# Linear attention and a multiplicative feed-forward on one core: w_out in four pieces, batch 0 first on two queues, and the whole sequence of steps as a list

## Chip, core and metric

The kernel runs on one core of a Trainium2 chip, in one launch. The metric is the device time in microseconds (us), from start to end of the program; lower is better. Each time of the kernel before is one execution; three were taken. The profile is of a fourth one.

## The reference

Eight batches of 8 heads, 576 tokens and 64 columns go through a linear attention, and its 4608 tokens of 512 columns through a feed-forward with no nonlinearity but one product:

```python
q_s = softmax(q, axis=head_dim)
k_s = softmax(k, axis=sequence)
kv  = einsum('bhsd,bhse->bhde', k_s, v)
x   = einsum('bhsd,bhde->bhse', q_s, kv)     # then (4608, 512)
h   = ((x @ w1) * (x @ w2)) @ w3             # 512 -> 1024 -> 1024
out = h @ w_out                              # 1024 -> 512
```

Everything comes in and goes out as float32.

## The kernel before

The kernel multiplies the two last weights first (W3O = w3 @ w_out, "the fold"), so each token needs only `x @ w1`, `x @ w2`, a product and one matmul with W3O. All matmuls are in float16.

**Steps.** The program is a set of named steps, each with one engine, a length and needs. `b` is a batch, `c` a chunk of 512 tokens (chunk 8 has the last 64 tokens of each batch), `p` one of two parts of the tokens of a batch (part 0 has 4 of 9 blocks, part 1 has 5), `hp` a pair of heads, `ft` one of 8 row blocks of w3.

- Loads: `k.b`, `q.b` (or `q.b.p`), `v.b`; `w3.r` (r = 0 to 3 one row block, 4 and 5 two each), `wo.i` (w_out), `w1.i` and `w2.i` (quarters of the columns). The loads that GpSimd (POOL) issues go through its own queue and cast the weights to float16; at most eight are under way, so each waits for the one eight before it. The others are issued by SyncE (SP), and in the kernel before one by ScalarE (ACT).
- Fold: `w3t.ft` (8 transposes on TensorE, PE), `w3T.ft` (copy to SBUF), `pf.ft.h` (matmuls with w_out, in pieces `h`), `W3O.ft` (scaled copy). Lines 430 to 455.
- Keys: `kmx` (max over tokens, on VectorE, DVE; as a tree of four max operations or as two reduces), `cb` (the max shared between partitions), `ksub`, `kexp`, `vc` (cast of v, batch 2 on), `kv` (matmuls), `kv2` (division).
- Queries: `qmx`, `qsub`, `qexp`, `qsm`, `qeps`, `qrc`, `qn`; then the transposed copy, by PE and a copy (`qt`, `qT`; batches 0 and 1) or by a DMA that transposes (`qd` on SP; batch 2 on). `xm`, `xt` are the matmuls with kv2, `xs`, `xts` their copies into the chunk's x.
- Feed-forward: `up.1` and `up.0` (x @ w2, x @ w1), `bs` (copy of the first to SBUF), `ab` (product, DVE), `down` (matmul with W3O), `os` (copy to SBUF), `st` (store, SP). Chunk 1 is done in two halves of 256 tokens.

**What sets the order.** `Plan` (lines 18 to 163) walks the steps with its own model: at each point it takes the engine that can begin first, and on it the ready step that is worth most, from the length of the chain behind it and a table of leads (`LEADS`). Each engine then executes its instructions in exactly this order: an instruction that waits holds all that come after it on its engine. `PICKS` says which engine does a step that two could do.

**Rings.** PSUM has four banks `pab` (w3t, up), two `po` (pf, down) and two `att` (the attention). A step that takes a bank waits until the one that had it before has been copied away. Two buffers `w3T`, four `osb` and four `bsb` go round in the same way.

**Ports.** For steps that the model puts before 50 us (`LINKED`), DVE and POOL steps that would want the same SBUF port are put one behind the other by hand (`link`).

**Start.** 35 matmuls on zeros (`WARM`, line 331) run ahead of the first real work on PE.

Of the kernel before, what the change touches and what calls it, by code (L numbers as in the profile page):

```python
# [17 lines left out]
class Plan:  # L18


    RATE = 409.0e3
# [3 lines left out]
    LINKED = 50.0  # L25
    BUS = 2.2
    BEGIN = {"SP": 0.74, "POOL": 1.25, "DVE": 1.0, "ACT": 0.74, "PE": 1.0}

    def __init__(self, rings, leads, picks):
        self.rings = rings  # L30
        self.leads = leads
        self.picks = picks
        self.steps = {}
# [53 lines left out]
    def order(self):  # L87
# [23 lines left out]
        order = []  # L111
        while ready:
            could = {}
            for s in ready:
# [17 lines left out]
            ready.remove(s)  # L132
            if s["takes"]:
                fifo[s["takes"]] += [s["name"]] * s["slots"]
# [30 lines left out]

LEADS = {
    "W3O_0": 3.86, "W3O_1": 96.54, "W3O_2": 83.51, "W3O_3": -17.88, "ab_0": -0.11, "ab_1": -73.36,
    "ab_3": 34.13, "bs_0": -13.75, "bs_1": 26.85, "cb_0": -28.89, "cb_1": -63.79, "cb_3": 85.84,
    "down_0": 18.28, "down_1": 46.89, "down_2": 9.08, "down_3": 7.55, "kexp_0": 74.7,
    "kexp_1": 91, "kexp_2": -24.67, "kexp_3": 36.31, "kmx_0": 45.3, "kmx_1": 45.3, "kmx_2": 3.5,  # L170
    "kmx_3": -326.21, "ksub_0": -8.7, "ksub_1": 43.5, "ksub_2": 11.41, "kv2_0": -31.5,
    "kv2_2": 9.92, "kv2_3": 9.95, "kv_0": -23.87, "kv_2": 73.56, "kv_3": 1.56, "os_0": 21,
    "os_1": 33.3, "pf_0": -14.77, "pf_1": -39.98, "qT_0": -24.5, "qT_1": 4.7, "qd_3": 74.8,
    "qeps_0": 28.2, "qeps_1": 75.9, "qeps_2": 37.85, "qeps_3": 10.34, "qexp_0": -32.3,
    "qexp_1": 16, "qexp_2": 53.74, "qmx_0": 53.9, "qmx_1": 35.3, "qmx_2": -27.61,
    "qmx_3": -327.82, "qn_0": 35, "qn_1": 67, "qn_2": 7.08, "qn_3": 52.76, "qrc_0": 4.6,
    "qrc_1": 72.9, "qrc_2": -5.55, "qrc_3": 10.13, "qsm_0": 39.4, "qsm_1": -10.4,
    "qsm_3": -119.37, "qsub_0": 33, "qsub_1": 46.8, "qsub_2": 4.33, "qsub_3": 56.82, "qt_0": 19.6,
    "qt_1": -23.5, "up0_0": -35.85, "up0_2": 29.56, "up0_3": 18.58, "up1_0": 34.45,
    "up1_1": -5.77, "up1_2": 83.41, "up1_3": 2.63, "vc_0": -11, "vc_1": 88.7, "vc_2": 14.71,  # L180
    "vc_3": -62.31, "w3T_1": -15.99, "w3T_2": -15.02, "w3T_3": 15.55, "w3t_0": 16.91,
    "w3t_1": -1.07, "w3t_2": 91.42, "w3t_3": -34.54, "xm_0": 13, "xm_1": 71, "xm_3": 40.96,
    "xs_0": -10.9, "xs_1": 40.6, "xs_2": -39.44, "xt_1": -8.76, "xt_2": 87.37, "xts_0": 92.5,
    "xts_1": 21.3, "xts_2": 20.18, "kexp_1_0": -3.8, "kmx_0_0": 35.13, "kmx_1_0": 10.95,
    "ksub_0_0": 67.6, "ksub_1_1": 98.9, "kv2_0_0": 66.1, "kv2_0_1": -22.4, "kv2_1_0": -4.2,
    "kv2_1_1": -2.9, "qT_0_0": -16.99, "qT_0_16": -45.54, "qT_1_16": 14.03, "qT_1_8": 84.36,
    "qeps_0_0": 62, "qeps_1_1": -9.58, "qexp_0_0": -10.92, "qexp_0_1": 44.82, "qexp_1_0": 37.04,
    "qexp_1_1": 87.94, "qmx_0_1": 81.93, "qmx_1_0": 3.1, "qmx_1_1": 40.66, "qn_0_1": 59.43,
    "qn_1_0": 17.44, "qrc_0_0": -5.67, "qrc_0_1": 56.34, "qrc_1_0": -35.48, "qrc_1_1": 61.9,
    "qsm_0_0": -32.45, "qsm_0_1": -0.84, "qsm_1_0": 111.27, "qsm_1_1": 32.24, "qsub_1_1": 51.26,  # L190
    "qt_0_8": 117.57, "qt_1_16": 50.48, "xm_0_0": -8.96, "xm_1_0": 37.69, "xs_0_0_0": 126.04,
    "xs_0_1_0": 22.27, "xs_1_0_0": 68.42, "xs_1_0_1": -20.74, "xs_1_1_0": -5.29,
    "xs_1_1_1": 24.82, "xts_0_0": 87.6, "xts_1_0": 44.57, "xts_1_1": 0.91, "pf_3": 93.65,
    "qt_1_8": 41.11, "xts_3": 61.7, "up0_1": -35.55, "xs_0_0_1": 38.71, "qd_2": -6.42,
    "qeps_1_0": 43.3, "xm_1_1": 15.9, "bs_3": 17.21, "ksub_3": 60.61, "kexp_0_1": -29.34,
    "xs_3": -18.62, "ksub_1_0": 40.77, "kv_1": -27.68, "qsm_2": -10.85, "os_3": 33.24,
    "qeps_0_1": -20.17, "qn_1_1": -32.16, "xt_0": -10.26, "w3T_0": 10.76, "kv2_1": -50.89,
    "pf_2": 21.11, "kexp_0_0": -3.81, "qT_1_0": 30.3, "qn_0_0": 8.76, "qt_0_0": -12.93,
    "qt_1_0": 70.46, "ab_2": 10.05, "qsub_0_1": 76, "xs_0_1_1": -39.93, "qT_0_8": 89.83,
    "xt_3": 59.16, "kexp_1_1": -11.89, "ksub_0_1": -14.41, "qexp_3": 1.21, "qmx_0_0": 70.49,  # L200
    "bs_2": 86.82, "cb_2": -45.47, "qsub_0_0": 70.81, "qsub_1_0": 31.62, "qt_0_16": -45.2,
    "xm_0_1": 58.68, "xts_0_1": 96.24,
# [36 lines left out]


LOADS = [
    ("q", 0, 1), ("q", 0, 0), ("w3", 4), ("wo", 0), ("k", 0), ("w3", 3), ("wo", 1), ("w3", 0),
    ("w3", 1), ("q", 1, 0), ("v", 0), ("w3", 5), ("k", 1), ("w3", 2), ("w2", 0), ("k", 2),
    ("w1", 0), ("w2", 2), ("w2", 1), ("w1", 1), ("w1", 2), ("v", 1), ("w1", 3), ("w2", 3),
    ("q", 1, 1),
]


@with_exitstack
def kernel(  # L250
    ctx: ExitStack,
    tc: tile.TileContext,
    q: bass.AP,
    k: bass.AP,
# [52 lines left out]
    st = {}  # L307
# [619 lines left out]
```

## Time and profile before

| what | value |
| --- | --- |
| median of 3 runs | 245.56 us (245.14 to 246.42) |
| the profiled execution | 246.21 us |
| its span, first to last instruction | 244.4 us |
| PE busy | 235.3 us (96%) |
| DVE, ACT, POOL busy | 177.2, 124.2, 118.9 us |
| PE at the head: matmuls on zeros | 1.55 to 12.06 us |
| first x @ w2 / first x @ w1 on PE | 37.62 / 38.93 us |

An engine's row in a timeline has the start, the length, the operation, and in brackets how long the engine was idle ahead of it and who ended this. "DMA to landing" is the time from the issue of a transfer to the end of it. The profiled execution is 1.8 us longer than its span, and 0.65 us above the median.

### The profile page before, as it was taken

The numbers are of one execution on the slowest core, as the hardware profiler recorded it, in microseconds if no ns is written. First come the engines' busy times: TensorE is split into PE (matmuls) and PEld (weight loads), VectorE is DVE, ScalarE is ACT, GpSimd is POOL, SyncE is SP. The second block draws the span as 40 slices with busy tenths as digits, with TensorE's granted clock in tenths as the row PEclk, the third lists the DMA queues.
The fourth block names the chain that finished last, engine by engine and source line by source line (L and its number), as shares of the span: only waits on it lengthen the run. The fifth ranks groups of instructions, "written<-read, shape, count | busy, mean of one in ns | idle before, by whom it ended". The sixth has DMA issues, their size and how long they took to land.

```text
span 244.4 us, 4841 instructions
## 1 busy us (share of the span) xinstructions
PE 235.3 (96%) x1919; PEld 115.1 (47%) x1919; DVE 177.2 (72%) x303; ACT 124.2 (51%) x189; POOL 118.9 (49%) x76
## 2 busy tenths in 40 slices
PE   7967999999999999999999999999999999999994
PEld 2444644457658344444444444444444344444443
DVE  0879799789889889898998899799965115573210
ACT  0374787468588357575565566655443612202221
POOL 8356789589791577086656646764470000000000
PEclk9999999999999999999999999999999999999999
DMA  6999999999999964985997299600830115000343
GB/s 206 266 253 251 305 299 199 240 371 352 395 401 232 215 132 144 398 152 117 339 317 153 46 361 326 150 14 4 188 80 3 43 43 130 1 0 0 87 130 129
DMA packets 37894, 45.66 MB, mean 187 GB/s; under 512 B 15984, under 2 KB 22384, under 8 KB 37872
## 3 DMA queue, kind: packets, MB, share of 16 engines
q1 hardware_dynamic: 29552, 33.69, 48.3%
q0 software_dynamic: 7792, 11.14, 20.7%
q10 hardware_dynamic: 528, 0.52, 0.6%
q8 instruction: 15, 0.25, 0.4%
q14 instruction: 7, 0.06, 0.1%
HBM read 38.80 MB, written 9.44 MB: 197 GB/s over the span
## 4 chain that ended last, share of the span: by engine, by line
PE 82%; DVE 5%; DMA 5%; POOL 4%; SPq 1%; ACT 1%; issue 1%; POOLq 0%; ACTq 0%
PE pab L786 48%; PE po L808 20%; PE po L444 4%; PE po L823 3%; PE pkv L555 2%; POOL en L620 2%; DMA q<-in_q_dram 2%; DMA qT<-en 2%; PE xm L661 2%; POOL q L588 2%; DVE q L588 1%; SPq L643 1%; DVE qm L583 1%; DVE qr L601 1%; PE w3t L434 1%
## 5 line engine op out<-in xcount | busy, mean ns | idle before, releaser
L801 DVE TENSOR_TENSOR ab<-pab,bsb 128x512 f16<-128x512 f32 x72 | 49.1, 686 | 29.4 <-PE pab L786 23.6
L786 PE MATMUL pab<-x,w2sb 128*128 128x512 f16 (+1 forms) x288 | 65.9, 356 | 0.0
L786 PE MATMUL pab<-x,w1sb 128*128 128x512 f16 (+1 forms) x288 | 65.9, 356 | 0.0
L808 PE MATMUL po<-W3O,ab 128*128 128x512 f16 x256 | 59.3, 380 | 0.0
L620 POOL TENSOR_TENSOR en<-eq,qr 128x1024 f16<-128x1024 f16 (+1 forms) x16 | 33.9, 2125 | 32.4 <-DVE qr L613 15.9
L342 ACT CAST bsb<-pab 128x512 f16<-128x512 f32 x42 | 24.6, 585 | 46.3 <-PE pab L786 36.8
L530 POOL TENSOR_TENSOR k<-k,cb 128x1152 f32<-128x1152 f32 x15 | 39.2, 2627 | 15.2 <-DVE cb L499 7.4
L786 PEld LDWEIGHTS <-w2sb 128*128 128x128 f16 x320 | 30.6, 98 | 29.9 <-issue 0.2
L786 PEld LDWEIGHTS <-w1sb 128*128 128x128 f16 x320 | 30.7, 98 | 29.5
L342 ACT COPY osb<-po 128x512 f32<-128x512 f32 (+1 forms) x33 | 19.1, 580 | 36.9 <-PE po L808 19.7
L808 PEld LDWEIGHTS <-ab 128*128 128x128 f16 x256 | 23.9, 98 | 29.3 <-issue 2.9
L588 POOL TENSOR_TENSOR q<-q,qm 128x1280 f32<-128x1280 f32 (+1 forms) x13 | 27.6, 2141 | 8.0 <-DVE qm L583 8.0
L342 DVE CAST bsb<-pab 128x512 f16<-128x512 f32 x30 | 20.4, 682 | 8.8 <-PE pab L786 7.8
L472 DVE TENSOR_REDUCE km<-k 128x128 f32<-128x1152 f32 x12 | 25.4, 2121 | 0.2 <-DMA k<-in_k_dram 0.2
L583 DVE TENSOR_REDUCE qm<-q 128x16 f32<-128x1024 f32 (+1 forms) x16 | 21.4, 1343 | 5.3 <-DMA q<-in_q_dram 5.2
L601 DVE TENSOR_REDUCE qr<-eq 128x16 f32<-128x1024 f16 (+1 forms) x16 | 21.2, 1329 | 2.4 <-ACT eq L596 2.4
L596 ACT ACTIVATE eq<-q 128x1024 f16<-128x1024 f32 (+1 forms) x16 | 18.6, 1164 | 5.6 <-POOL q L588 4.4
L538 ACT ACTIVATE ek<-k 128x1152 f16<-128x1152 f32 x16 | 18.6, 1165 | 5.5 <-POOL k L530 3.0
L346 ACT ACTIVATE x<-xm 128x512 f16<-128x512 f32 x29 | 16.2, 596 | 6.9 <-PE xm L661 6.8
L444 PE MATMUL po<-wosb,w3T 128*128 128x512 f16 x64 | 15.3, 380 | 2.0 <-ACT w3T L342 1.6
L342 ACT CAST v<-v 128x1152 f16<-128x1152 f32 x11 | 12.4, 1162 | 2.3 <-DMA v<-in_v_dram 2.3
L368 PE MATMUL idle<-zero 128*128 128x512 f16 x35 | 10.5, 475 | 1.6 <-DVE zero L365 1.6
(62 smaller groups left out, 166.7 us busy)
## 6 DMA issues: line engine op xcount, KB each, us to landing
out_dram<-osb SPq DMA_DIRECT2D x66, 128.0 KB, 2.5
q<-in_q_dram SPq DMA_DIRECT2D x6, 1152.0 KB, 9.2
v<-in_v_dram SPq DMA_DIRECT2D x6, 1152.0 KB, 11.6
k<-in_k_dram SPq DMA_DIRECT2D x5, 1152.0 KB, 5.5
k<-in_k_dram POOLq DMA_DIRECT2D x3, 1152.0 KB, 11.8
v<-in_v_dram POOLq DMA_DIRECT2D x2, 576.0 KB, 14.9
w<-in_moe_w_dram POOLq DMA_DIRECT2D x2, 512.0 KB, 11.9
wosb<-in_moe_w_out_dram POOLq DMA_DIRECT2D x2, 512.0 KB, 11.7
```

The source lines that it names most:

```text
L342: return [(nc.scalar.copy if eng == "ACT" else engine[eng].tensor_copy)(out=out, in_=in_)]
L444: nc.tensor.matmul(st["pf", ft], lhsT=st["w3T", ft][:, gt, :], rhs=wosb[:, gt, :], start=(gt == 0), stop=(gt == N_FT - 1))
L472: dve.tensor_reduce(out=st["km", b][:, two(hp), :], in_=kb[:, two(hp), :, :].rearrange("p h j d -> p h d j"), axis=AX.X, op=ALU.max)
L530: return [engine[eng].tensor_tensor(out=kb[:, two(hp), :, :], in0=kb[:, two(hp), :, :], in1=st["cb", b][:, two(hp), None, :].broadcast_to( ...
L538: nc.scalar.activation(out=st["ek", b][:, hp, :, :].rearrange("p j (i d) -> p i j d", i=2), in_=kb[:, two(hp), :, :], func=AF.Exp)
L583: dve.tensor_reduce(out=st["qm", b][:, :, j], in_=qb[:, :, j, :], axis=AX.X, op=ALU.max)
L588: return [engine[eng].tensor_tensor(out=qb[:, :, j, :], in0=qb[:, :, j, :], in1=st["qm", b][:, :, j, None].broadcast_to([P, HH, n, D]), op ...
L601: dve.tensor_reduce(out=st["qr", b][:, :, slice(*PARTS[p])], in_=st["eq", b, p], axis=AX.X, op=ALU.add)
L620: return [engine[eng].tensor_tensor(out=st["en", b][:, j, :, :].rearrange("p j h d -> p h j d"), in0=st["eq", b, p], in1=st["qr", b][:, :, ...
L786: nc.tensor.matmul(st["p", one, c, sub, u][:, a * (t1 - t0):(a + 1) * (t1 - t0)], lhsT=w[:, ct, fb * P:(fb + 1) * P], rhs=x()[:, ct, t0:t1 ...
L801: dve.tensor_tensor(out=st["ab", c][:, nf * u:nf * u + nf, t0:t1], in0=cut(st["p", 0, c, sub, u]), in1=cut(st["bsb", c, sub, u]), op=ALU.mult)
L808: nc.tensor.matmul(st["po", c, tb], lhsT=st["ab", c][:, ft, tb * P:(tb + 1) * P], rhs=W3O[:, ft, :], start=(ft == 0), stop=(ft == N_FT - 1))
```

## The change

- **w_out** comes in four pieces (`WOS = 4`), and a row block of the fold in four quarters of two matmuls. Its accumulator is in `po` for even and in `pab` for odd blocks.
- **k and q of batch 0**: `k.0` and `q.0.0` are split by heads into halves, one from SP and one from ACT. `q.0.1` goes to POOL's queue. The other loads of POOL have a new order, and `k.2` is the last of them; `q.2` on SP still waits for the third last of the list, now `w2.3`.
- **The sequence** of all 788 steps is written out in `ORDER`; the model only takes the next name. `LEADS` loses its use for the order, and many `PICKS` change: of the copies `bs`, 30 were on DVE and now one is, the others are on ACT.
- Batches 2 and 3 take `kmx` as a tree too (`TREES` 2 to 4), and `link` holds to 60 us.
- **24 matmuls on zeros** in place of 35.

```diff
-    def __init__(self, rings, leads, picks):
+    def __init__(self, rings, leads, picks, first):
...
+        self.first = [tuple(int(x) if x.isdigit() else x for x in n.split(".")) for n in first.split()]
...
+        listed = [steps[n] for n in self.first]
         while ready:
             could = {}
-            for s in ready:
+            for s in listed[:1] or ready:
+                assert not s["open"], s["name"]
...
+            listed = listed[1:]
...
+ORDER = """
+k.0 q.0.0 w3.4 wo.2 wo.1 wo.0 w3.5 wo.3 q.0.1 w3.2 ident kmx.0.0 qmx.0.0 w3.0 w3t.4 cb.0 w3t.5
+qsub.0.0 w3T.4 w3T.5 v.0 ksub.0.1 qexp.0.0 w3.3 pf.4.0 k.1 qsm.0.0 pf.5.0 pf.4.1 pf.5.1 ksub.0.0
+pf.4.2 pf.5.2 w3.1 w3t.7 qeps.0.0 kexp.0.0 qrc.0.0 w3t.6 qn.0.0 q.1.0 pf.4.3 pf.5.3 w3T.6 qt.0.0
+qmx.0.1 q.1.1 W3O.4 pf.6.0 pf.6.1 W3O.5 pf.6.2 w3T.7 w2.0 pf.6.3 qsub.0.1 w3t.2 kexp.0.1 pf.7.0
+w1.0 pf.7.1 w3T.2 pf.7.2 qexp.0.1 w3t.0 pf.2.0 pf.7.3 qT.0.0 qsm.0.1 pf.2.1 w2.1 pf.2.2 W3O.6
+kv.0 w3T.0 qeps.0.1 qrc.0.1 qn.0.1 pf.2.3 W3O.7 kv2.0 pf.0.0 w3t.3 W3O.2 pf.0.1 w3T.3 pf.0.2 w1.1
+qt.0.16 qt.0.8 kmx.1.0 qT.0.16 w2.2 pf.0.3 qT.0.8 pf.3.0 w1.3 w3t.1 pf.3.1 w3T.1 xm.0.0 w1.2
+pf.3.2 xs.0.0.0 xs.0.0.1 pf.3.3 pf.1.0 qmx.1.0 W3O.3 xm.0.1 w2.3 pf.1.1 xs.0.1.1 pf.1.2 xs.0.1.0
+qsub.1.0 pf.1.3 qmx.1.1 up.1.0.0.0 xt.0 bs.0.0.0 up.0.0.0.0 v.1 cb.1 W3O.1 up.1.0.0.1 qsub.1.1
+qexp.1.0 up.0.0.0.1 bs.0.0.1 ab.0.0.0 up.1.0.0.2 ab.0.0.1 ksub.1.0 qexp.1.1 up.0.0.0.2 qsm.1.0
+up.1.0.0.3 bs.0.0.2 xts.0.1 up.0.0.0.3 qeps.1.0 xts.0.0 ab.0.0.2 bs.0.0.3 ksub.1.1 up.1.0.0.4
+kexp.1.0 qsm.1.1 up.0.0.0.4 W3O.0 q.2 ab.0.0.3 up.1.0.0.5 bs.0.0.4 v.2 k.2 ab.0.0.4 up.0.0.0.5
+bs.0.0.5 qrc.1.0 kexp.1.1 up.1.0.0.6 qn.1.0 up.0.0.0.6 bs.0.0.6 k.3 qeps.1.1 ab.0.0.5 q.3 qt.1.0
+qrc.1.1 up.1.0.0.7 qT.1.0 ab.0.0.6 qn.1.1 up.0.0.0.7 bs.0.0.7 qmx.2.1 kv.1 ab.0.0.7 down.0.0
+qsub.2.1 qmx.2.0 vc.2.1 down.0.1 kv2.1 qsub.2.0 qexp.2.1 os.0.0 xm.1.0 xs.1.0.0 st.0.0 down.0.2
+qsm.2.1 vc.2.0 xs.1.0.1 os.0.1 up.1.1.0.0 kmx.2.0 st.0.1 qt.1.8 down.0.3 v.3 qT.1.8 qexp.2.0
+qeps.2.1 up.0.1.0.0 qrc.2.1 cb.2 qn.2.1 qt.1.16 up.1.1.0.1 qT.1.16 bs.1.0.0 xm.1.1 bs.1.0.1
+up.0.1.0.1 ab.1.0.0 ksub.2.1 qd.2.1 up.1.1.0.2 ab.1.0.1 xs.1.1.0 xs.1.1.1 os.0.2 up.0.1.0.2
+qsm.2.0 st.0.2 up.1.1.0.3 bs.1.0.2 ksub.2.0 kexp.2.1 up.0.1.0.3 ab.1.0.2 qmx.3.0 up.1.1.1.0
+qeps.2.0 bs.1.0.3 up.0.1.1.0 ab.1.0.3 qsub.3.0 up.1.1.1.1 kexp.2.0 qmx.3.1 up.0.1.1.1 bs.1.1.0
+k.4 kv.2 qrc.2.0 bs.1.1.1 ab.1.1.0 qn.2.0 qexp.3.0 up.1.1.1.2 kv2.2 up.0.1.1.2 vc.3.1 ab.1.1.1
+xt.1 qd.2.0 down.1.0 qsm.3.0 xts.1.0 os.0.3 q.4 kmx.3.0 qeps.3.0 v.4 xts.1.1 up.1.1.1.3 bs.1.1.2
+up.0.1.1.3 os.1.0 bs.1.1.3 xm.2.1 down.1.1 xs.2.1.1 qrc.3.0 st.1.0 qsub.3.1 xs.2.1.0 vc.3.0
...
+"""
...
 LOADS = [
-    ("q", 0, 1), ("q", 0, 0), ("w3", 4), ("wo", 0), ("k", 0), ("w3", 3), ("wo", 1), ("w3", 0),
-    ("w3", 1), ("q", 1, 0), ("v", 0), ("w3", 5), ("k", 1), ("w3", 2), ("w2", 0), ("k", 2),
-    ("w1", 0), ("w2", 2), ("w2", 1), ("w1", 1), ("w1", 2), ("v", 1), ("w1", 3), ("w2", 3),
-    ("q", 1, 1),
+    ("k", 0), ("q", 0, 0), ("w3", 4), ("wo", 2), ("wo", 1), ("wo", 0), ("w3", 5), ("wo", 3),
+    ("q", 0, 1), ("w3", 2), ("w3", 0), ("v", 0), ("w3", 3), ("k", 1), ("w3", 1), ("q", 1, 0),
+    ("q", 1, 1), ("w2", 0), ("w1", 0), ("w2", 1), ("w1", 1), ("w2", 2), ("w1", 3), ("w1", 2),
+    ("w2", 3), ("v", 1), ("k", 2),
 ]
...
-    TREES = 2
+    TREES = 4
...
-    WARM = 35
+    WARM = 24
...
-            st[name] = {"SP": nc.sync, "ACT": nc.scalar, "POOL": g_}[queue].dma_start(out=dst, in_=src)
+            if name in LOADS and queue == "SP":
+                h = HH // 2
+                nc.sync.dma_start(out=dst[:, :h], in_=src[:, :h])
+                nc.scalar.dma_start(out=dst[:, h:], in_=src[:, h:])
+                return
+            st[name] = (nc.sync if queue == "SP" else g_).dma_start(out=dst, in_=src)
...
+        ring = ("po", "pab")[ft % 2]
+
         def mm(h):
             if not h:
-                st["pf", ft] = p_o()
-            for gt in range(h * N_FT // 2, (h + 1) * N_FT // 2):
+                st["pf", ft] = p_ab() if ft % 2 else p_o()
+            for gt in range(h * N_FT // WOS, (h + 1) * N_FT // WOS):
```

## The prediction, made before the changed kernel ran

> **What bounds the kernel now.** First the page's busy times, then PE's row of busy time by stage:
>
> ```profile
> PE 235.3 (96%) x1919; PEld 115.1 (47%) x1919; DVE 177.2 (72%) x303; ACT 124.2 (51%) x189; POOL 118.9 (49%) x76
> ...
> 60.00:90.00 30.00, 29.48 (x279) 17.52 (x278) 26.24 (x45) 18.63 (x30) 18.68 (x10) 1.00 1.05 294
> 90.00:120.00 30.00, 30.00 (x287) 13.62 (x286) 26.87 (x48) 18.31 (x26) 19.58 (x9) 1.00 0.71 205
> ```
>
> From 22.2 us to 241.1 us PE (first number after the length) stands still for 0.52 us in all. The real PE work is the same in both kernels (11 matmuls on zeros less is all that differs), so the time can change only where PE idles: ahead of 22.2, in that 0.52, in waits that the new order makes, or after the last matmul, where nothing changes. PE's timeline shows the idle places:
>
> ```profile
> 1.55 10.51 PE L368 MATMUL idle<-zero 128*128 128x512 f16 x35 [1.55 <-DVE zero L365]
> 11.89 1.15 PE L434 MATMUL w3t<-ident,w 128*128 128x128 f16 x16
> 13.65 1.04 PE L444 MATMUL po<-wosb,w3T 128*128 128x512 f16 x4 [0.61 <-ACT w3T L342]
> 15.73 1.04 PE L444 MATMUL po<-wosb,w3T 128*128 128x512 f16 x4 [1.04 <-ACT w3T L342]
> ...
> 22.21 0.73 PE L635 MATMUL qtp<-ident,en 128*128 128x128 f16 x10 [1.80 <-POOL en L620]
> ...
> 37.62 1.03 PE L786 MATMUL pab<-x,w2sb 128*128 128x512 f16 x4
> ...
> 38.93 1.03 PE L786 MATMUL pab<-x,w1sb 128*128 128x512 f16 x4
> ...
> 81.37 0.41 PE L661 MATMUL xm<-qT,kv 64*64 64x512 f16 x4 [0.52 <-DMA qT<-en]
> ```
>
> Last the transfers, one at a time with issue and time to landing. Here `q.2`, and ACT's cast `vc.2.1`, which waits for `v.2`:
>
> ```profile
> L400 SPq DMA_DIRECT2D q<-in_q_dram x1: 385/385/385, 47.4 to 47.4; - x1
> ...
> DMA to landing us min/median/max: 6.5/6.5/6.5
> ...
> 57.51 1.15 ACT L342 CAST v<-v 128x1152 f16<-128x1152 f32 x1 [0.53 <-DMA v<-in_v_dram]
> ```
>
> Issue plus time to landing gives (us): `q.0` 6.6, `w3.4` 9.0, `wo.0` 11.5, `k.0` 14.5, `wo.1` 18.0, `w3.0` 19.3, `v.0` 25.3, `w3.5` 27.8, `k.1` 30.8, `w1.0` 37.8, `v.1` 46.0, `w1.3` 47.3, `w2.3` 48.7, `q.1.1` 50.3, `q.2` 53.9, `v.2` 57.5, `k.3` 60.4. The transfers come one behind the other without a hole; each takes 1.3 (0.52 MB read), 1.6 (`q.1.1`), 2.5 (1.05 MB) or 2.9 to 3.6 us (a whole k, q or v).
>
> **The change, part by part.**
>
> *Landings.* With this pace and the new order: `k.0` 6.6 (same bytes and queues as `q.0` before), `q.0.0` 8 to 9, `w3.4` 10.25 (9.0 plus 1.3 for `q.0.0`, which is now ahead), `wo.2`, `wo.1`, `wo.0` 11.5, 12.8, 14.05, `w3.5` 16.5, `wo.3` 17.8, `q.0.1` 19.4, `w3.2` 20.7, `w3.0` 22.0, `v.0` 25.2, `w3.3` 26.4, `k.1` 29.4, `w3.1` 30.7, `q.1.0` 32.0, `q.1.1` 33.6, `w2.0` 34.9, `w1.0` 36.2, `w2.1` to `w2.3` every 1.3 up to 44.0, `v.1` 46.9. Check: before, `w2.3` came at 48.7; without `k.2` (3.3) and `v.1` (2.9) and with `q.1.1` (1.6) ahead it comes at 44.1.
>
> *Zeros.* Eleven fewer. The first 13 start 0.427 apart (to 7.1), the others 0.214, so 24 end at 9.45. Nothing waited for them; no gain by itself.
>
> *PE up to the first x @ w1.* `w3t.4`, `w3t.5` 10.25 to 11.3 (0.5 each). `pf` needs `wo.0`: idle to 14.05; three quarters of two blocks (12 matmuls of 0.216) to 16.65; `w3t.7`, `w3t.6` (`w3.5` is there) to 17.65; wait for `wo.3`, last quarters 17.9 to 18.8; `qt.0.0` to 19.2. Here the two `w3T` buffers turn round: `w3T.6` after `pf.4.3` on ACT (1.01) 18.5 to 19.5, so `pf.6` 19.55 to 21.3; `w3t.2`, three quarters of `pf.7`, `w3t.0`, `pf` to 25.3; `kv.0` (`v.0` at 25.2) to 26.75; `pf`, `w3t.3` to 29.0; `qt.0.16`, `qt.0.8` to 29.6. Their input is the long chain: `q.0.1` 19.4, `qmx` 1.48, `qsub` 1.49, `qexp` 1.27, `qsm` 1.49, 0.5, `qn` on POOL 2.33: 28.2, covered by 0.8. `w3t.1` waits for `w3.1` to 30.8 (0.35); `xm.0` and the last `pf` to 35.2; `up.1.0.0.0` 35.2 (`w2.0` 34.9), `up.0.0.0.0` 36.3 (`w1.0` 36.2).
>
> Before, `up.0.0.0.0` began at 38.93 with 22.28 us of work done, idle (or on zeros) 16.65; now 36.3 with 22.01 (`qt.1.0` comes later), 14.3. **Head: -2.35 us.** The first `pf` is not earlier (13.65 before); what goes are the waits of 0.6, 1.0 and 1.8 us and the zeros up to 12. Bounds: pace 5% off moves `w1.0` by 1.7, so -0.7 to -3.5; I keep -2.35, since the check above lies within 0.1.
>
> *Chunk 0.* 16 ups, `qt.1.0`, `kv.1`: each weight is there (`w1.2` at 42.7 for 43.2 is the closest), `v.1` by 3 us. Without a wait `down.0.0` begins at 51.4 and `up.1.1.0.0`, the first of chunk 1, at 57.05 (20.4 us of work after 36.3 and 0.35 of switching, as between 38.93 and 58.52 before).
>
> *Batch 2, the place where it is decided.* PE is 2.35 earlier, but the bytes are the same. `q.2` is issued when `w2.3` lands (44.1), `v.2` right behind it on SP's queue; `k.2`, which was in at 36.6, is now issued by POOL at 44.7 (after `qsub.1.0` 1.9, `qsub.1.1` 2.3, `ksub.1` 2 x 2.64, from 34.4). So three whole tensors come after `v.1` on two queues: `q.2` from 46.5, and from about 48 `k.2` beside `q.2` and `v.2`. Three transfers took 10.1 us before (50.3 to 60.4). `v.2` bounds: 53.2 if SP's queue goes first (46.9 + 2 x 3.2), 57.0 if it is last of the three. No row shows both queues loaded alike; nearest is `q.1.1`, which took its usual 1.6 us with `q.2` waiting: POOL's queue does not stand back. I take equal shares: `q.2` 50.6 to 52, `k.2` and `v.2` together, `v.2` 56.0.
>
> The Trainium skill ("DMA: Bandwidth & Descriptors", section "Queues, rings and completion order") says that each DMA engine goes round robin, packet by packet, between the queues that have work. By that rule `v.2` comes at about 56 too, and not in the order of issue that the plan counts on, which speaks against the change.
>
> What waits for `v.2`: on ACT the order is `bs.0.0.7`, `vc.2.1`, `qexp.2.1`, `xs.1.0.0`, `xs.1.0.1`, `os.0.1`. `vc.2.1` (1.16), `qexp.2.1` (1.27) and two `xs` (1.1) with hops are 3.7 us from landing to the x that `up.1.1.0.0` needs: 59.7. Before, these stood behind other work at 57.5 to 59.8, with PE 40.7 us into its work (now 42.4 at this place). A second wait, `qmx.2.1` on DVE for `q.2`, holds `ab.0.0.7`, `kv2.1` and `os.0.0`: 0 to 0.85, hidden under the first. So `up.1.1.0.0` starts 2.65 late, and -2.35 becomes +0.3.
>
> *`xm.2`.* `kmx.2` (now 2.8 as a tree) runs on DVE between `qsm.2.1` and `qrc.2.1`, then POOL in order: `qn.2.1` from 63.5, `ksub.2` 5.3, `qsub.3.0`, `qn.2.0` to 74.9, `qd.2.0` behind `k.4` (issued 72.5; `k.5` alone took 5.3: 77.8). Transposes landed 3.2 to 3.5 us after issue when alone, and 4.1 after the load ahead of them when not: 78.4 to 81.9, near the first, say 80. `xm.2.1` would begin at 79.4: wait 0.6. The old wait of 0.52 is gone with its place.
>
> *Copies to ACT, trees.* 29 `bs` of 0.585 add 17 us to ACT, which has 18.3 of 30 busy in the stage above; DVE loses 20 and 3 more by the trees (2.83 against two of 2.15, twice). Nobody waits for either there; if ACT's cover were gone, PE would wait at the fifth `pab` bank. 0, bounds -0.3 to +1: PE cannot gain where it has no idle time.
>
> **Sum** against the profiled execution: 246.21 - 2.35 + 2.65 + 0.6 - 0.52 = 246.6; minus 0.65, as that execution lies above its median: 245.9. As `q.2` may come at its early end and `v.2` at 55.6 (1.18 MB shared from 48), the terms lean down: I say **245.7**, its own range 244.5 to 246.8.
>
> **Rivals.**
>
> *SP's queue goes first* (30%). For it: at the start, `q.0` on SP and ACT landed at 6.6 and POOL's `w3.4`, issued 0.5 us later, needed 2.4 more, its whole own time. Against: `q.1.1` above. Then `v.2` is at 53.2, `up.1.1.0.0` starts at 57.4, and -2.35 keeps all but 0.35, with a wait of 0 to 1.5 at `xm.2.1` against 0.52: 243.0 to 244.9, at best 243.6.
>
> *`qd.2.0` lands late* (22%, slower). Mechanism: SP's transposing DMA sits in the ring behind `k.4`, with `q.4` after it. For it: before, with loads about, the two took 10.0 and 5.7 us from issue. Against: 3.2 to 3.5 for batch 3. Place `xm.2.1`; it decides from landing at 81.0 on (79.4 plus 1.6). At 82 to 83, PE waits 2.6 to 3.6, and the time is 247.6, up to 248.5.
>
> *The head does not bring it* (4%): PE idles from 11.3 to 14.05 and begins slow again, as at the start (0.427 for 5.5 us): 2.75 later, less about 1.0 of waits that take it up. Under late `v.2` it costs nothing; with early `v.2` it gives 245.2. In the trace a gap of 1.8 us did not slow PE.
>
> The Trainium skill ("TensorE: Matmul & The Clock Gate", "Part 1: The HAM clock gate") has PE's clock halved after an idle window of about 3.4 us, longer than this gap; no run here shows that limit.
>
> **Chances and range.** Forecast 44%, first rival 30%, slower rival 22%, the slow head 4%. About 0.5% (1.2 us) is what a measurement of this kernel can tell from no change: faster below 244.3, slower above 246.8. The first rival is mostly faster (26 of 30), the forecast's low edge adds 3; the slower rival gives 22 and the forecast's upper edge 3; the rest is within. Range: 243.3 leaves the best of the first rival out, 247.5 half of the slower one.
>
> **What would show it.** Right: first `pf` at 14, `up.0.0.0.0` near 36.3, then PE idle ahead of the first up of chunk 1 with ACT `vc` ended by DMA v at 55 to 57. Wrong: no idle PE between 50 and 62 (first rival), a wait above 2 at `xm` for DMA qT (slower rival), or PE waits for ACT's `bs` after 90, which I put at nothing.

## The result: 3.1 us slower

The changed kernel takes 248.66 us (median of four runs, 248.48 to 248.94) against 245.51 for the kernel before in the same rounds: ratio 1.0124, 95% interval 1.0094 to 1.0153. That is slower by 1.2%, clear of the noise, and above the forecast of 245.7 and the upper end of its range, 247.5. The profiled execution took 248.94, its span is 247.2 (before: 246.21 and 244.4). One execution of run 7 below, 344.57 us at a mean granted clock of 0.658, is left out of that run's median and ratio.

The page after: the busy times, and in tenths of the span the TensorE clock that was granted.

```profile
PE 235.5 (95%) x1908; PEld 115.0 (47%) x1908; DVE 156.2 (63%) x278; ACT 140.5 (57%) x219; POOL 117.7 (48%) x77
...
PEclk9959999999999999999999999999999999999999
```

PE has 235.5 us of busy time for 235.3 before, with 11 matmuls less. DVE lost 21 us and ACT gained 16, as the copies moved. The third slice of the clock row, 12.4 to 18.5 us, shows a 5: the clock was halved there. The first window below shows the same stretch; the columns are window, length, then busy time of PE, PEld, DVE, ACT, POOL with counts, granted clock, DMA share, GB/s:

```profile
12.00:18.00 6.00, 4.27 (x11) 1.48 (x11) 5.72 (x11) 2.62 (x3) 3.92 (x6) 0.56 1.11 254
...
60.00:90.00 30.00, 28.21 (x292) 18.81 (x292) 25.93 (x50) 21.99 (x38) 19.22 (x9) 1.00 0.87 248
```

From 60 to 90 us PE is busy 28.21 us, where it had 29.48, with ACT at 21.99 for 18.63: the waits that follow lie there. PE's timeline, the rows that carry the result:

```profile
9.97 1.18 PE L485 MATMUL w3t<-ident,w 128*128 128x128 f16 x16 [0.91 <-DMA w<-in_moe_w_dram]
13.73 1.01 PE L497 MATMUL po<-wosb,w3T 128*128 128x512 f16 x2 [2.57 <-DMA wosb<-in_moe_w_out_dram]
...
38.35 1.04 PE L839 MATMUL pab<-x,w1sb 128*128 128x512 f16 x4
...
60.67 0.27 PE L839 MATMUL pab<-x,w2sb 128*128 128x256 f16 x1 [1.57 <-ACT x L392]
...
61.15 0.92 PE L839 MATMUL pab<-x,w2sb 128*128 128x256 f16 x7 [0.22 <-ACT x L392]
...
81.64 0.41 PE L718 MATMUL xm<-qT,kv 64*64 64x512 f16 x4 [0.90 <-DMA qT<-en]
...
156.03 1.02 PE L839 MATMUL pab<-x,w1sb 128*128 128x512 f16 x4 [0.44 <-DVE ab L854]
```

The first `pf` starts at 13.73, as predicted (14), but two matmuls take 1.01 where they take 0.59 at the full clock. So the first x@w1 stands at 38.35, not 36.3. Then PE waits four times: 1.57 and 0.22 for the x of chunk 1, 0.90 for `qd.2.0`, 0.44 for an `ab`. ACT's timeline and the chain of waits (start, length, what) say why x was late:

```profile
57.81 1.16 ACT L388 CAST v<-v 128x1152 f16<-128x1152 f32 x1 [6.07 <-DMA v<-in_v_dram]
58.87 1.26 ACT L653 ACTIVATE eq<-q 128x1280 f16<-128x1280 f32 x1
60.04 1.06 ACT L392 ACTIVATE x<-xm 128x512 f16<-128x512 f32 x2
```

```profile
45.45 12.33 DMA v<-in_v_dram
```

ACT stands still for 6.07 us in front of the cast `vc.2.1`, because `v.2` lands at 57.8; the x that PE needs is copied behind it.

**The account**, between the ends of the last matmuls (241.13 and 243.95, +2.82): the head gives -0.31 (38.93 to 38.35, with 0.27 us less of work done by then); the x of chunk 1 +1.79; `xm.2.1` +0.38 (0.90 for 0.52); `ab` at 156 +0.44. The other 0.52 is not idle time: from the first x@w1 to the end PE is idle for 3.13 us, which is the four waits together. It lies in PE's busy time, 202.47 us for 201.68 before (0.27 of the difference is the work that moved), and is not explained here.

### The profile page after: what moved, and what is told of

It is laid out like the page before. It is cut to its first block, busy times and chain, and to the rows that moved or that the text cites. A ratio compares the mean times of both kernels' runs of the same rounds, so it can differ in the third digit from the quotient of the medians.

```text
span 247.2 us, 4830 instructions
## 1 busy us (share of the span) xinstructions
PE 235.5 (95%) x1908; PEld 115.0 (47%) x1908; DVE 156.2 (63%) x278; ACT 140.5 (57%) x219; POOL 117.7 (48%) x77
## 4 chain that ended last, share of the span: by engine, by line
PE 69%; DMA 15%; POOL 4%; DVE 3%; ACT 3%; issue 2%; SPq 2%; ACTq 0%; POOLq 0%; DVEq 0%
PE pab L839 37%; PE po L861 17%; DMA v<-in_v_dram 5%; DMA wosb<-in_moe_w_out_dram 4%; DMA q<-in_q_dram 4%; PE po L497 3%; PE pab L497 3%; PE po L876 3%; DMA qT<-en 2%; POOL en L677 2%; PE xm L718 2%; PE pkv L612 2%; PE w3t L485 1%; POOL k L587 1%; DVE qm L640 1%
## 5 line engine op out<-in xcount | busy, mean ns | idle before, releaser
L388 ACT CAST bsb<-pab 128x512 f16<-128x512 f32 x71 | 41.3, 584 | 35.3 <-PE pab L839 34.9
L677 POOL TENSOR_TENSOR en<-eq,qr 128x1280 f16<-128x1280 f16 (+1 forms) x14 | 30.2, 2154 | 34.8 <-DVE qr L670 18.7
L587 POOL TENSOR_TENSOR k<-k,cb 128x1152 f32<-128x1152 f32 x14 | 36.6, 2632 | 12.1 <-DVE cb L556 8.8
L388 ACT COPY osb<-po 128x512 f32<-128x512 f32 (+1 forms) x35 | 20.0, 576 | 26.9 <-PE po L861 22.0
L645 POOL TENSOR_TENSOR q<-q,qm 128x1024 f32<-128x1024 f32 (+1 forms) x15 | 31.6, 2113 | 4.6 <-DVE qm L640 4.5
L529 DVE TENSOR_REDUCE km<-k 128x128 f32<-128x1152 f32 x8 | 17.3, 2161 | 0.0
L388 ACT COPY w3T<-w3t 128x1024 f16<-128x1024 f16 x7 | 7.0, 1022 | 12.6 <-PE w3t L485 10.0
L497 PE MATMUL po<-wosb,w3T 128*128 128x512 f16 x32 | 9.9, 426 | 2.9 <-DMA wosb<-in_moe_w_out_dram 2.6
L497 PEld LDWEIGHTS <-w3T 128*128 128x128 f16 x64 | 6.2, 106 | 10.1 <-issue 4.8
```

The costliest lines, as they stand in the source:

```text
L388: return [(nc.scalar.copy if eng == "ACT" else engine[eng].tensor_copy)(out=out, in_=in_)]
L497: nc.tensor.matmul(st["pf", ft], lhsT=st["w3T", ft][:, gt, :], rhs=wosb[:, gt, :], start=(gt == 0), stop=(gt == N_FT - 1))
L587: return [engine[eng].tensor_tensor(out=kb[:, two(hp), :, :], in0=kb[:, two(hp), :, :], in1=st["cb", b][:, two(hp), None, :].broadcast_to( ...
L645: return [engine[eng].tensor_tensor(out=qb[:, :, j, :], in0=qb[:, :, j, :], in1=st["qm", b][:, :, j, None].broadcast_to([P, HH, n, D]), op ...
L677: return [engine[eng].tensor_tensor(out=st["en", b][:, j, :, :].rearrange("p j h d -> p h j d"), in0=st["eq", b, p], in1=st["qr", b][:, :, ...
```

## The experiments

Each is the changed kernel with the edit shown. Names that move in `ORDER` are shown alone, with their new neighbours.

### 1 to 4: the four suspects one at a time

**Run 1: 35 zeros, as before.**

```diff
-    WARM = 24
+    WARM = 35
```

> The changed kernel with 35 matmuls on zeros again. Both theories expect PE's clock at full from 13.7 us on, the first x @ w1 near 36.5 us (38.35 without). Theory A (the end is set by v.2's landing, 57.8 us, through ACT's vc.2.1): the wait ahead of up.1.1.0.0 grows from 1.8 to about 3.6 us and the time stays at 248.7 (248.2 to 249.0). Theory B (the slow clock is what costs): 246.7.

248.41 us (1.0114, 1.0087 to 1.0140), as theory A said. The first x@w1 came at 37.27, 1.08 earlier, but `up.1.1.0.0` started at 60.65 as before: PE waited 0.49 for `ab.0.0.7` and 1.80 and 0.22 for x. The clock still fell, at 14.70, for one stretch of 3.41 us where the changed kernel had 6.83. That, and not the zeros by themselves, goes with the 1.08 us: the traces of runs 6 and 8, with 24 zeros and one such stretch, have the first x@w1 at 37.34 and 37.31. Fewer zeros are not the loss.

**Run 2: work in the gap.** Twelve more matmuls on zeros stand where PE waits for `wo.0`.

```diff
+            if (ft, h) == (4, 0):
+                for i in range(12):
+                    nc.tensor.matmul(idle, lhsT=zero[:, 0:P], rhs=zero, start=True, stop=True)
```

> The changed kernel with 24 zeros at the start and 12 more between w3t.5 and pf.4.0, where PE stands still for 2.57 us. If the gap is what slows the clock, pf runs at 0.216 us from 13.7 on and the first x @ w1 is near 36.5; if the number of zeros at the start is, PE stays slow to 19 and x @ w1 starts at 38.3. Time: A 248.7 in both cases, B 246.7 in the first.

249.05 us (1.0135, 1.0116 to 1.0153). PE's timeline of this run:

```profile
11.02 2.75 PE L496 MATMUL idle<-zero 128*128 128x512 f16 x12
13.74 0.59 PE L500 MATMUL po<-wosb,w3T 128*128 128x512 f16 x2
...
36.54 1.04 PE L842 MATMUL pab<-x,w1sb 128*128 128x512 f16 x4
...
54.07 2.12 PE L864 MATMUL po<-W3O,ab 128*128 128x512 f16 x9 [0.91 <-DVE ab L857]
...
60.58 0.27 PE L842 MATMUL pab<-x,w2sb 128*128 128x256 f16 x1 [2.04 <-ACT x L392]
```

In the profiled execution the clock stays full and the first x@w1 stands at 36.54, near the 36.3 of the prediction. The time does not move: the head's 1.81 us becomes a wait of 0.91 for `ab.0.0.7` and a longer one for x, which is copied at 59.95 as it was at 60.04. By their mean granted clock, two of the four executions kept the full clock (1.000: 248.59 and 248.89 us) and two had one halved stretch (0.993: 249.20 and 249.33); the first two, too, are no faster than the changed kernel. So the slow clock is real, and it is not what made the kernel slower.

**Run 3: the cast of v.2 behind os.0.1.**

```diff
-... qmx.2.0 vc.2.1 down.0.1 ...
+... qmx.2.0 down.0.1 ...
-... os.0.1 up.1.1.0.0 ...
+... os.0.1 vc.2.1 up.1.1.0.0 ...
```

> The changed kernel with vc.2.1 behind os.0.1 on ACT, nothing else. Theory A: xs.1.0 no longer stand behind the wait for v.2, so the wait of 1.8 us ahead of up.1.1.0.0 goes (0 to 0.3 left), qexp.2.1 comes 2.4 earlier, and the wait of 0.9 at xm.2.1 falls to 0.2 or so: 246.2 (245.8 to 247.0). Theory B, or a DMA bound that strikes elsewhere: 248.4 or more.

246.28 us (1.0024, 1.0007 to 1.0041): 2.4 us from one name. ACT's timeline of this run has the copies of x at 57.32 and the cast behind them, and PE does not wait for x at all:

```profile
57.32 1.08 ACT L391 ACTIVATE x<-xm 128x512 f16<-128x512 f32 x2 [1.52 <-PE xm L717]
...
58.76 1.18 ACT L387 CAST v<-v 128x1152 f16<-128x1152 f32 x1
```

The wait at `xm.2.1` fell to 0.24 with it. This is the main cause, shown by taking it away.

**Run 4: k.2 issued behind qn.1.1**, so that POOL's queue leaves the transfers to SP's.

```diff
-... q.2 ab.0.0.3 ... v.2 k.2 ab.0.0.4 ...
+... qn.1.1 k.2 up.0.0.0.7 ...
```

> The changed kernel with k.2 issued by POOL after qn.1.1 (about 52 us in place of 46.3). If the two queues share the transfer time, v.2 lands near 54.5 in place of 57.8, vc.2.1 is done before xs.1.0 are due, and the time is 246.2 (245.8 to 247.2). If SP's queue is not held up by POOL's, v.2 and the time stay (248.7). If k.2 is then too late for kmx.2, the wait moves to xm.2.1 and the time is 247.5 or more.

250.02 us (1.0173, 1.0142 to 1.0205). ACT, DVE and PE of this run:

```profile
54.71 1.15 ACT L387 CAST v<-v 128x1152 f16<-128x1152 f32 x1 [2.98 <-DMA v<-in_v_dram]
```

```profile
62.81 1.23 DVE L537 TENSOR_TENSOR kmx<-k 128x1024 f32<-128x1024 f32 x1 [4.26 <-DMA k<-in_k_dram]
```

```profile
68.83 1.03 PE L838 MATMUL pab<-x,w2sb 128*128 128x256 f16 x8 [1.77 <-DVE ab L853]
```

`v.2` lands 3.1 us earlier when `k.2` does not share with it, and the wait for x is gone; now `kmx.2` and `cb.2` wait for `k.2` on DVE, with `ab` behind them, and that costs more. The bytes were only passed on. The sharing also agrees with the rule of the Trainium skill that the prediction cited from "DMA: Bandwidth & Descriptors", "Queues, rings and completion order".

### 5 to 9: where the head's gain goes

**Run 5: runs 2 and 3 together.**

> This run joins the two edits tried alone: the 12 matmuls on zeros in the wait for the first piece of w_out (which brought the first x@w1 from 38.35 to 36.54), and vc.2.1 listed behind os.0.1 (which alone gave 246.28). Theory A (a chain of bounds in batch 2: behind the cast stands DVE's column of k.2, whose first step waits for vc.2.0 on POOL and so again for v.2's landing near 57.75; it ends near 64.3 whatever the head does, and ab.1.0.0 stands behind it): the 1.8 us that the head gains turns into a wait of PE for ab of 1.0 to 1.6 near 64, and of the rest for qd.2.0 at xm.2.1; 245.6 to 246.3. Theory B (nothing else is near): the head's 1.8 us comes through whole, 244.5.

246.44 us (1.0040, 1.0020 to 1.0061): no better than run 3, though the first x@w1 is 1.7 earlier (36.69). The total is just above the 245.6 to 246.3 of the theory of a chain of bounds, and 1.9 above the other's; but the main wait is not where it was put. PE's timeline:

```profile
54.42 2.12 PE L864 MATMUL po<-W3O,ab 128*128 128x512 f16 x9 [1.11 <-DVE ab L857]
```

`ab.0.0.7` stands on DVE behind `qmx.2.1`, which waits 3.39 for `q.2`. About 0.7 of the rest was lost at `xm.2.1`.

**Run 6: batch 2 listed anew, the head as it is.**

```diff
-... qmx.2.0 vc.2.1 down.0.1 ... vc.2.0 xs.1.0.1 os.0.1 up.1.1.0.0 kmx.2.0 ...
+... qmx.2.0 down.0.1 ... xs.1.0.1 os.0.1 vc.2.1 up.1.1.0.0 kmx.2.0 vc.2.0 ...
-... ab.1.0.3 qsub.3.0 ... k.4 kv.2 qrc.2.0 ... qn.2.0 ... qd.2.0 ...
+... ab.1.0.3 qrc.2.0 qn.2.0 qd.2.0 qsub.3.0 ... k.4 kv.2 ...
```

> Only the listing of batch 2 is changed, the head is left as it is with its slow clock: vc.2.1 behind os.0.1, vc.2.0 behind kmx.2.0 (so that DVE's column of k.2 waits for k.2's landing near 57.0 alone), and qrc.2.0, qn.2.0, qd.2.0 ahead of qsub.3.0 and k.4. Theory A: without the head's gain PE asks for these results as late as in the run with vc.2.1 alone (246.28), where the waits near 65 and at xm.2.1 were 0.2 and 0.24; so 245.8 to 246.3, and qd.2.0 lands near 75 where it landed at 78.9. Theory B (the batch-2 chain still costs by itself what the change lost): 244.5.

245.50 us (1.0005, 0.9993 to 1.0018), between the two theories: 0.3 under A's 245.8 to 246.3 and 1.0 above B's 244.5. No wait of PE is left between the fold and 152 us; there it waits 0.77 for an `ab`. So what the change lost against the kernel before could be had back in the listing of batch 2 alone, with the slow head left as it is.

**Run 7: run 6 with w_out's pieces in the order 0, 1, 2, 3.**

```diff
-    ("k", 0), ("q", 0, 0), ("w3", 4), ("wo", 2), ("wo", 1), ("wo", 0), ("w3", 5), ("wo", 3),
+    ("k", 0), ("q", 0, 0), ("w3", 4), ("wo", 0), ("wo", 1), ("wo", 2), ("w3", 5), ("wo", 3),
```

> As the run before it, and the pieces of w_out are loaded in the order 0, 1, 2, 3, where the change has 2, 1, 0, 3: the fold's first matmuls need piece 0 and can start near 12.0 instead of 13.73, so PE has no long pause. Theory A (the pause of 2.57 is what lowers the clock, and the head's gain is worth something only when the listing of batch 2 lets it through): the clock stays full, the first x@w1 stands near 36.5, and the time is 1.8 under the run before it: 244.0 to 244.5, under the kernel before. Theory B (the clock falls for another reason, as the total of activity): first x@w1 at 38.3 and 246. Theory C (the head gains but another wait of batch 1 or 2 takes it): first x@w1 at 36.5 and 245.5 to 246.

246.43 us (1.0032, 1.0012 to 1.0052), its profiled execution 245.24. Theory A failed twice. In the profiled execution the clock fell although PE's longest pause was now 1.25:

```profile
10.14 1.19 PE L485 MATMUL w3t<-ident,w 128*128 128x128 f16 x16 [1.25 <-DMA w<-in_moe_w_dram]
...
12.87 1.04 PE L497 MATMUL pab<-wosb,w3T 128*128 128x512 f16 x2 [0.31 <-ACT w3T L388]
```

And the 0.6 us that the head gained (36.71) went into a wait of 0.76 for `ab.0.0.7` at 54.1, as in run 5. Six of the other executions kept the clock (mean 0.999 or 1.000); they took 245.81 to 246.84, where theory A had 244.0 to 244.5.

**Run 8: run 6 with kmx.6.1 ahead of qmx.7.1**, for the wait near 152 to 156.

> As the run with only batch 2's listing changed (245.50), and kmx.6.1 listed ahead of qmx.7.1, so that DVE does it in its 2.64 us of waiting for q.7 instead of behind it. Theory A (that wait of DVE is what makes PE wait 0.77 at 152.4 and 0.44 at 156.0 in the changed kernel): the only wait of PE behind the fold is gone, 244.7. Theory B (PE's stall moves to the next step behind q.7): 245.3 to 245.6.

245.92 us (0.9994, 0.9973 to 1.0015), a little above what theory B said. ACT and PE of this run:

```profile
152.25 1.27 ACT L653 ACTIVATE eq<-q 128x1280 f16<-128x1280 f32 x1 [2.80 <-POOL q L645]
```

```profile
154.05 1.02 PE L839 MATMUL pab<-x,w2sb 128*128 128x512 f16 x4 [0.95 <-ACT bsb L388]
```

DVE no longer holds `ab`, but ACT now stands 2.80 us in front of `qexp.7.1`, with `bs.5.0.1` behind it. Both wait for the same transfer, `q.7`. The trace is of an execution with one halved stretch. Three of the twelve, at a mean clock of 0.986 (two stretches), took 244.66 to 244.91, the time of theory A; they have no trace, and why they were faster is open.

**Run 9: all of it, and 30 zeros.**

> All in one: the run before it, and for the head 30 matmuls on zeros and w_out's pieces in the order 0, 1, 2, 3, so that the time between the last matmul on zeros (about 9.9) and the fold's first (about 12.0) is 2.0 with 16 transposes in it; and, so that the head's gain isn't stopped by q.2's landing, ab.0.0.7 ahead of qmx.2.1, kv2.1 and os.0.0 ahead of qmx.2.0, xs.1.0.0 and xs.1.0.1 ahead of qexp.2.1, kmx.2.0 ahead of qsm.2.1, bs.1.0.0 and ab.1.0.0 ahead of cb.2. Theory A (the clock falls some 3.4 to 4 us after the last full matmul when only transposes and waits lie between, as the runs with 3.07 and 4.2 to 4.7 between showed and the run with 2.6 did not): the fold runs at full rate, the first x@w1 stands at 36.3 to 36.6, up.1.1.0.0 near 57.2 without a wait, 243.6 to 244.0. Theory B (transposes are not the reason, the clock falls again): first x@w1 at 36.7 to 37.4; 244.2 to 244.7.

246.47 us (1.0024, 1.0009 to 1.0038), where theory A had 243.6 to 244.0. The clock stayed full in all twelve executions, as theory A had it, and `up.1.1.0.0` stood at 57.46 without a wait. But with `qsm.2.1` and `ab.1.0.0` between `kmx.2.0` and it, `cb.2` ended at 66.7 instead of 63.8 (run 6), and PE waited 0.84, 0.69 and 0.34 between 67 and 72. A better head, a worse batch 2.

### 10 to 12: a version under both kernels, and the clock

**Runs 10 and 11: the same batch 2, with the slow and with the full head.** Beside run 6:

```diff
-... bs.0.0.7 qmx.2.1 kv.1 ab.0.0.7 ...
+... bs.0.0.7 ab.0.0.7 qmx.2.1 kv.1 ...
-"xs_1_0_0": "ACT", "xs_1_0_1": "ACT", "os_0_0": "DVE"
+"xs_1_0_0": "DVE", "xs_1_0_1": "DVE", "os_0_0": "ACT"
+... os.0.0 qexp.2.1 ... xs.1.0.1 qsm.2.1 ... bs.1.0.0 qexp.2.0 ... ab.1.0.0 cb.2 ...
+... kmx.6.1 qmx.7.1 ... bs.5.0.1 qexp.7.1 ...
```

Run 11 has run 7's order of w_out and `WARM = 30` besides.

> The head as the change has it (24 zeros, pieces 2, 1, 0, 3, slow clock); of batch 2 the listing that gave 245.50, and in it ab.0.0.7 ahead of qmx.2.1, os.0.0 on ACT, xs.1.0.0 and xs.1.0.1 on DVE behind kv2.1, bs.1.0.0 ahead of qexp.2.0, ab.1.0.0 ahead of cb.2; near 150 kmx.6.1 ahead of qmx.7.1 and qexp.7.1 behind bs.5.0.1, so that neither DVE's nor ACT's wait for q.7 stands before PE. Theory A (PE's stall of 0.8 to 1.0 there is a matter of the listing): no wait of PE behind the fold; 244.6 to 244.9. Theory B (it moves on once more): 245.4 to 245.7.

> The run before it with the head that kept the clock: 30 zeros, pieces in the order 0, 1, 2, 3. The two differ in the head alone. Theory A (with nothing late behind it the slow clock costs what it takes from the head): first x@w1 near 36.4 to 36.6, where the other has 37.3 to 38.4, and the time 0.8 to 1.8 under the other: 243.2 to 244.0, under the kernel before. Theory B (another wait in batch 2 takes the head's gain, as in every run so far): PE waits again between 54 and 80, and the time is that of the other run.

Run 10: 245.45 us (0.9997, 0.9982 to 1.0011); the longest wait of PE behind the fold is 0.24, so the stall near 150 was a matter of the listing, as theory A had it, but the total is theory B's: it gained 0.05 over run 6, not the 0.6 or more expected. Run 11: **244.68 us (0.9954, 0.9938 to 0.9970)**, under the kernel before. PE's timeline of run 11:

```profile
12.32 0.61 PE L497 MATMUL po<-wosb,w3T 128*128 128x512 f16 x2 [0.62 <-ACT w3T L388]
...
35.64 1.04 PE L839 MATMUL pab<-x,w2sb 128*128 128x512 f16 x4 [0.38 <-DMA w2sb<-in_moe_w_dram]
...
36.96 1.04 PE L839 MATMUL pab<-x,w1sb 128*128 128x512 f16 x4
```

In the profiled executions the first x@w1 is 0.64 earlier than in run 10 (37.60), and the median is 0.77 lower: with nothing late behind it, the head's gain comes through. It is just under the 0.8 to 1.8 expected: the trace of run 10 had less of its fold under the slow clock (to 17.94) than the changed kernel, and run 11's head now waits for `w2.0`.

**Run 12: transposes in the gap.** As run 2, with 40 transposes of zeros for the 12 matmuls.

> As the run with 12 matmuls on zeros in the wait for the first piece of w_out (there the clock stayed full, the first x@w1 stood at 36.54 and the time stayed at 249.05), but with 40 transposes of zeros (128 columns each) in their place, so that PE is as little idle, without a full matmul between about 9 and 13.7. Theory A (transposes don't count as work for the clock): the granted clock falls to 0.50 all the same, for 3.4 or 6.8 us, and the first x@w1 stands at 37.3 to 38.4. Theory B (it is PE's idle time that counts): the clock stays at 1.00, first x@w1 near 36.5. In both the time is 248.4 to 249.1, as v.2 sets it.

248.78 us (1.0122, 1.0056 to 1.0189). Theory B: the clock stayed at 1.00 and the first x@w1 stood at 36.80; the other of the two executions kept the clock too. So 40 transposes held the clock up here, as 12 matmuls did in run 2.

## Why the prediction was wrong, step by step

The sum said 246.6 for the profiled execution, which took 248.94. Of the 2.3 us missed, 1.2 are at the first up of chunk 1, 0.3 at `xm.2.1`, 0.44 at 156 us, and 0.4 have no row.

- **Landings, zeros, first pf**: right. `w1.0` landed at 36.8 (36.2 said), `v.1` at 47.7 (46.9), the zeros ended at 9.06 (9.45), `pf` began at 13.73.
- **Head, -2.35**: failed, but it is not what made the time; -0.31 was measured. What failed in it is "three quarters of two blocks (12 matmuls of 0.216)": they were 0.427 apart. The third rival, with a chance of 4%, was what happened, in the manner it described, and so was its clause "under late `v.2` it costs nothing" (run 2). Its argument against, that a gap of 1.8 us had not slowed PE, was the wrong measure (last section).
- **v.2, the term of 2.65**: this is the step that failed and set the time, since run 2 mended the head and left the time at 249.05, while run 3 took this wait away and gave 246.28. The mechanism was right to the instruction, the size was not. Net of the head the prediction had +0.30 at this place; +1.48 was measured. `v.2` landed at 57.8, not 56.0; from there to the first up of chunk 1 it took 2.9, not 3.7, so that this up began at 60.67, not 59.7. The bytes say so without any model of queues: three whole tensors follow `v.1`, and three took 10.1 us before and 10.1 now (47.7 to 57.8). Two of them were on SP's queue and one on POOL's, and the last to land was SP's (`q.2` 51.2, `k.2` 57.1, `v.2` 57.8). The prediction had 57.0 as its bound for this very case and took a middle value; it then leaned the sum down once more.
- **First rival, SP's queue first** (30%): refuted. `v.2` came at 54.7 only when `k.2` was held back (run 4).
- **ab.0.0.7 behind q.2, "0 to 0.85, hidden"**: right as long as x is later; with a faster head it was a bound of its own, 0.91, 1.11 and 0.76 in runs 2, 5 and 7.
- **xm.2.1, 0.6 in place of 0.52**: 0.90. `qd.2.0` was issued at 76.26 and landed at 81.6; said were about 80 and, for the slower rival, 81.0 and later. It did come right behind `k.4` (80.8), as that rival had it. PE's need had moved later too, so the slower rival did not decide: slower came by `v.2`, a wait in the forecast itself.
- **Copies and trees, 0**: no wait for a `bs` or a `pab` bank came of them alone. The wait at 156 did come from the new order, through `qmx.7.1` and `kmx.6.1` in front of `ab.5.0.0` on DVE. The prediction has no term for this place: it works out nothing of the list behind batch 3. It should have looked for every place where an instruction that waits for a load stands ahead of a `bs` or `ab`.

## What to carry to other kernels

When a hand-written order puts an instruction that waits for a transfer ahead of one that the bottleneck engine needs, that transfer's landing sets the time, and what is gained ahead of it is waited away: here one name moved by 13 places was worth 2.4 us, and up to 1.8 us gained in the head were worth nothing until the places behind it were mended too. To size the landing, count the bytes queued up to it on all queues and divide by the pace of the trace; in both kernels here the last of three tensors came 10.1 us after the load ahead of them. Mend the places in the order of time, since each hides the next.

## What the runs showed of the clock

The clock changed on a fixed grid. The records of the granted clock in the traces have it halved from 12.78 to 19.61 in the changed kernel (6.83 us), and in run 7 from 12.44 to 15.85 (3.41); runs 1, 6 and 8 gave 3.41, and runs 3, 4 and 10 gave 6.83. The clock had come up at 5.95 in the changed kernel, where the matmuls on zeros go from 0.427 us apart to 0.216, and it fell 6.83 us later; in run 1 it came up at 4.46 and fell 10.24 later. These lengths are one, two and three times 3.413 us, so a stretch begins a whole number of them after the rise. The rise itself came at 4.29 in run 10 and at 7.30 in run 6, which have the same head: each execution meets the stretches at another place.

In the stretch of 3.41 just ahead of each fall PE had been busy for half of the time or less. The windows of the changed kernel, of run 7, and of run 12, which kept the clock:

```profile
9.37:12.78 3.41, 1.18 (x16) 1.14 (x17) 2.81 (x9) 1.93 (x2) 2.25 (x2) 1.00 1.13 210
```

```profile
9.03:12.44 3.41, 1.67 (x18) 1.17 (x18) 2.40 (x6) 1.55 (x2) 1.75 (x2) 1.00 1.13 211
```

```profile
8.00:11.41 3.41, 1.68 (x24) 1.35 (x23) 2.67 (x6) 0.60 (x1) 1.04 (x2) 1.00 1.13 217
```

PE (first number after the length) was busy 1.18 and 1.67 us ahead of the two falls; 0.86, 1.31 and 1.68 in runs 6, 1 and 10, and 1.21, 1.18 and 0.85 in runs 3, 4 and 8. In the profiled executions of runs 2, 5, 9, 11 and 12 and of the kernel before, which kept the clock, no stretch of 3.41 begun between 8.0 and 17.8 had less than 1.68. So a pause need not be long: pauses of 1.25 and 0.62 with transposes between them were enough in run 7, and PE's work in the stretch decides, near one half of it, by these runs. The exact bound was not settled: run 1 kept the clock through the stretch from 59.07 to 62.48 with 1.61. To bring the clock back took more: with 2.46 us of work in the stretch from 12.78 to 16.19 it stayed down in the changed kernel, and the least with which it rose was 2.74 (run 10, 0.87 to 4.29).

Only one execution of each kernel has a trace, but the mean granted clock of all is known; one halved stretch makes it about 0.993, two about 0.986. With the head of the change as it is (the changed kernel, runs 3, 4, 6, 8 and 10) it was 0.993 or less in all 53 executions. In runs 1 and 2 that was so in two of four each, in run 5 in one of ten, in run 7 in five of eleven, and in runs 9, 11 and 12 in none of twenty.

The Trainium skill ("TensorE: Matmul & The Clock Gate", "Part 1: The HAM clock gate") gives a free-running window of 3413 ns; the lengths of 3.41 and 6.83 agree. It names an idle window as the condition, and there the measurement decides: no window ahead of a fall was idle here, PE was busy for 0.85 to 1.68 us of it.
